# Attention in a fused kernel: 224 instead of 160 columns of one exponential as a polynomial, its value product one pair later

## The chip, the cores and the metric

The kernel runs on one core of a Trainium2 chip. The metric is device time in microseconds (us): the median of three runs before the change is 1327.5 us (1327.15 to 1327.72). A core has TensorE (PE in the profile; PEld is its weight load), VectorE (DVE), ScalarE (ACT), GpSimd (POOL) and SyncE (SP, which here only issues DMAs). SBUF is the working memory, PSUM the memory that matmuls write to.

## The reference, cut to what matters

```python
def reference(A_x, A_wqkv, A_wo, B_x, B_w_gate, B_w1, B_w2, gate_w):
    # a: 16 heads of width 28 over 2048 positions
    scores = jnp.einsum("bhqd,bhkd->bhqk", q, k) * scale
    p = _softmax(scores, axis=-1)
    o = jnp.einsum("bhqk,bhkd->bhqd", p, v)
    a = o.transpose(0, 2, 1, 3).reshape(B, S, D) @ wo
    # b: eight experts, the two best for each position
    b = _B_ref(x, B_w_gate, B_w1, B_w2)
    g = _sigmoid((x * gate_w).sum(-1, keepdims=True))
    return g * a + (1 - g) * b
```

Everything is float32. The change touches only `p` and the product of `p` and `v`.

## The kernel before, in words

The kernel first makes queries, keys and values and routes the positions, then runs the experts (with the row maxima of the scores between), then the attention, then the output projection. The change lies in the attention, which begins at about 829 us of the span and ends at about 1287 us.

**Units and pairs.** Sixteen units `u`, one for each group of four heads and each quarter of 512 queries (`NU = 16`). A unit goes over the 16 tiles of 128 keys in eight pairs `p` (`NPR = 8`). All is numbered by `m = 8u + p`, 0 to 127. The loop (L1377) calls for each `m`: `scores(m + 1)`, `values(m)`, then `beside(m)`, which puts smaller work between: DMAs, splitting the projection's weights (`split_wo_high`, `split_wo_low` in units 5 to 8 at p = 0 to 3), the reciprocals of the row sums, and in the last unit the splitting of the output. A manual schedule holds PE, VectorE, ScalarE and GpSimd to the order in which the code issues; each works through its own queue in that order.

**Scores.** `scores` makes, for both key tiles of a pair and four heads, a 128 x 512 block of scores, in three passes of four matmuls (`score_passes`, L796), the four on different rows of the array. The four blocks of the first tile go to the bank z0 and the three banks s0, those of the second to s1 (three) and z1. PSUM has just these eight banks, and `values` uses z0 and z1 again: its two accumulators are `single(0)` and `single(1)`. So the next scores of the first tile need z0 after the first addition of `values`, and those of the second tile need z1 after the second.

**Exponentials.** Eight blocks of 512 columns for each pair. ScalarE does one from z0 (L1276), three from s0 (L1277) and three from s1 (L1285). The eighth block, z1, is first scaled by VectorE into `X` (L1278); ScalarE then makes the exponential of its first 512 - 160 = 352 columns (L1286), and `power` makes the other 160 as a polynomial: GpSimd forms u, n, g and the exponent bits e (L1292, L1293, L1294, L1297), VectorE y, v, w and the last product (L1301, L1302, L1303, L1305). GpSimd also issues DMAs from the lists `due` and `rows`: of these one comes before e and one behind it.

**Values.** `values(m)` multiplies the eight blocks with the values, first the columns 0 to 287 (`CA = 288`) of all blocks, then 288 to 511, each of the four heads on its own 32 columns of the array: 8 + 8 matmuls (L1319), each of which appears twice in the trace, since float32 takes two instructions. VectorE adds the first part to the unit's sums (`add0` in what follows, L1331, or a copy at p = 0, L1329), then the second (`add1`). Between them stands `piece`: in units 2 to 15 at p = 2 and 3 half of the division of an earlier unit (L1205).

Of the kernel before, what the change touches and what calls it, by code (L numbers as in the profile page):

```python
# [9 lines left out]
F32 = mybir.dt.float32  # L10
# [3 lines left out]
AF = mybir.ActivationFunctionType  # L14
ALU = mybir.AluOpType
# [22 lines left out]
NT = S // 128  # L38
# [12 lines left out]
SCALE = float(DH) ** -0.5  # L51
# [13 lines left out]
def tile_gated_mha_moe(ctx: ExitStack, tc: tile.TileContext, x, xe_, xT, wv, wqk, wo, w1, w2, out):  # L65
    nc = tc.nc
# [31 lines left out]
    DATA = mybir.DependencyInfo(mybir.DependencyClass.Sync, mybir.DependencyReason.DATA)  # L98
# [127 lines left out]
    def whole(n):  # L226
        return -(-n // 32) * 32
# [69 lines left out]
    with ExitStack() as pa:  # L297
        sb = pa.enter_context(tc.tile_pool(name="pa_sb", bufs=1))
# [119 lines left out]
        for t in range(NT):  # L418
# [368 lines left out]
    Ps = {}  # L787
# [13 lines left out]
    with ExitStack() as pb:  # L801
        sb1 = pb.enter_context(tc.tile_pool(name="pb_sb1", bufs=2, reuse_waits="tile"))
        sb = pb.enter_context(tc.tile_pool(name="pb_sb", bufs=2, reuse_waits="tile"))
# [175 lines left out]
        for e in range(E):  # L979
# [11 lines left out]
            for hf in range(2):  # L991
# [3 lines left out]
                for f in range(NH):  # L995
                    ft = hf * NH + f
                    p = e * NP + ft // 2
# [73 lines left out]
                for n_k, k in enumerate((4, 0, 1, 2, 3)):  # L1071
# [7 lines left out]
                    n = min(128, CAPS[e] - k * 128)  # L1079
                    cs = slice(k * 128, k * 128 + n)  # L1080
                    if k < 4:
                        py = accumulator()
                    i = 0
                    for f in range(NH if k < 4 else 0):
                        hh, hl, ht = hs[f]
                        w2h, w2l, w2r = w2t[base + f]
                        for a, b in ((hh, w2h), (hh, w2l), (hl, w2h)):
                            mm = nc.tensor.matmul(py[:n, 0:D], a[:, cs], b, start=i == 0, stop=i == 3 * NH - 1)  # L1088
# [7 lines left out]
                        if hf == 1 and e + 1 < E and (f == 1 or f == 4 and n_k == 1):  # L1096
                            j = n_k if f == 1 and n_k > 1 else f // 4
# [30 lines left out]
    sb = ctx.enter_context(tc.tile_pool(name="pc_sb", bufs=2, reuse_waits="tile"))  # L1128
# [100 lines left out]

    ctx.enter_context(tc.manual_schedule(engines=MANUAL_E))  # L1230
    NPR = NT // 2
    PW = 160
    CA = 288
    ROUND = 1.5 * 2.0 ** 23
    LAM = 0.3125
    EXP2 = (-1.4162444446908184, 1.4393188497873604, 0.43138228078296503, 0.3791024559194178)
    powers = {}
    due, rows = [], []
    NU = 4 * NG
    b1s, halves = {}, {}  # L1240
    accs, rc, rs = {}, {}, {}
    qs = {0: q, 1: load_q(0, 1)}
    held = {0: (kts, v1)}
    Pc = {0: Ps[0] + Ps[1]}

    arrivals = {}
    def behind_values(u, p):
# [4 lines left out]
    def single(i):  # L1252
        return ps.tile([128, 512], F32, name=f"z{i % 2}")
# [9 lines left out]
    def scores(m):  # L1263
        u, p = divmod(m, NPR)
        if p == 0 and u and u + 1 < NU:
            qs[u + 1] = load_q((u + 1) // 4, (u + 1) % 4)
            behind_values(u, 5)
        X = sb.tile([128, 512], F32, name="X")
        P = sb.tile([128, 8, 512], F32, name="P")
        z, t = [None] * 2, [None] * 2  # L1270
        for i in range(2):
            kt = 2 * p + i
            z[i], t[i] = single(i), triple(i)
            three = [t[i][:, j] for j in range(3)]
            score_passes(kt, held[u // 4][0][kt // 8], qs[u], three + [z[i]] if i else [z[i]] + three)
        nc.scalar.activation(P[:, 0], z[0], AF.Exp, scale=SCALE)  # L1276
        nc.scalar.activation(P[:, 1:4], t[0], AF.Exp, scale=SCALE)  # L1277
        nc.vector.tensor_scalar(X, z[1], LAM * SCALE * math.log2(math.e), -126.0 * LAM, op0=ALU.mult, op1=ALU.max)  # L1278
        if m - 1 in powers:
            next(powers.pop(m - 1), None)  # L1280
        w = PW if m + 1 < NU * NPR else 0
        if w:
            powers[m] = power(X[:, 512 - w:], P[:, 7, 512 - w:])
            next(powers[m])
        nc.scalar.activation(P[:, 4:7], t[1], AF.Exp, scale=SCALE)  # L1285
        nc.scalar.activation(P[:, 7, 0:512 - w], X[:, 0:512 - w], AF.Exp, scale=math.log(2.0) / LAM)  # L1286
        Pc[m] = [P[:, i] for i in range(8)]

    def power(x, to):
        u, n, g, y = (sb.tile([128, PW], F32, name=f"p{c}", bufs=1 + (c == "u")) for c in "ungy")  # L1290
        e, v, w = u.bitcast(I32), x, g
        nc.gpsimd.tensor_scalar(u, x, 1.0 / LAM, ROUND, op0=ALU.mult, op1=ALU.add)  # L1292
        nc.gpsimd.tensor_scalar(n, u, -ROUND, LAM, op0=ALU.add, op1=ALU.mult)  # L1293
        nc.gpsimd.tensor_tensor(g, n, x, op=ALU.subtract)  # L1294
        if due:
            due.pop(0)()
        nc.gpsimd.tensor_scalar(e, u, 127.0 - ROUND, 2.0 ** 23, op0=ALU.add, op1=ALU.mult)  # L1297
        if rows:
            rows.pop(0)()
        yield  # L1300
        nc.vector.scalar_tensor_tensor(y, g, EXP2[0], g, op0=ALU.add, op1=ALU.mult)  # L1301
        nc.vector.scalar_tensor_tensor(v, y, EXP2[1], g, op0=ALU.add, op1=ALU.add)  # L1302
        nc.vector.scalar_tensor_tensor(w, y, EXP2[2], v, op0=ALU.add, op1=ALU.mult)  # L1303
        yield
        nc.vector.scalar_tensor_tensor(to, w, EXP2[3], e.bitcast(F32), op0=ALU.add, op1=ALU.mult)  # L1305

    def values(m):
        u, p = divmod(m, NPR)
        P = Pc.pop(m)
        parts = [(single(0), slice(0, CA)), (single(1), slice(CA, 512))]  # L1310
        runs = [(n, i) for n in range(2) for i in range(2)]
        if m + 1 == NU * NPR:
            runs.sort(key=lambda r: r[1])
        for n, i in runs:
            po, cs = parts[n]
            kt = 2 * p + i
            v = held[u // 4][1][kt // 8]
            for j in range(4):
                mm = nc.tensor.matmul(po[32 * j:32 * j + 32, cs], v[:, kt % 8, 32 * j:32 * j + 32],  # L1319
                                      P[4 * i + j][:, cs], start=i == 0, stop=i == 1)  # L1320
                if arrivals.get(m) and (i, j) not in ((0, 0), (1, 3)):
                    tc.add_manual_dep(mm.ins, arrivals[m].pop(0).ins.name, DATA, reason="operands' arrival")
        if p == 0:
            accs[u] = sb.tile([128, 512], F32, name="osb", bufs=4)
        for n, (po, cs) in enumerate(parts):
            if n:
                piece(u, p)
            if p == 0:
                nc.vector.tensor_copy(accs[u][:, cs], po[:, cs])  # L1329
            else:  # L1330
                nc.vector.tensor_tensor(accs[u][:, cs], po[:, cs], accs[u][:, cs], op=ALU.add)  # L1331

    def piece(u, p):
        if u > 1 and p in (2, 3):
            divide_half(u - 2, p - 2)
# [41 lines left out]
    for m in range(NU * NPR):  # L1377
        if m + 1 < NU * NPR:
            scores(m + 1)
        values(m)  # L1380
        u, p = divmod(m, NPR)
        if u + 1 < NU and p in (4, 6):
            rows.append(lambda t=u + 1, c=p // 2 - 2: fetch_routed(t, c))
        if u == 0 and p in (0, 2):
            rows.append(lambda t=u, c=p // 2: fetch_routed(t, c))
        beside(m)
        if m + 1 in powers:
            next(powers[m + 1])
    collect_sums(NU - 1)
    slice_sums(NU - 1)  # L1390
    divide(NU - 2)
# [3 lines left out]
    for t in range(NT):  # L1395
# [67 lines left out]
```

## Time and profile before

| | us |
|---|---|
| median of three runs | 1327.5 |
| lowest, highest | 1327.15, 1327.72 |
| the profiled execution: its own time | 1328.14 |
| its span, first to last instruction | 1326.3 |
| PE, PEld busy | 1321.1, 928.2 |
| VectorE, ScalarE, GpSimd busy | 1068.2, 838.3, 858.1 |

The profiled execution is 0.64 us above the median, and 1.8 us of its time lie outside the span. A row that groups instructions gives the engine, the operation, out<-in by the program's names, the shapes, the count, then the busy time, the mean in ns, and the idle time of the engine just before them with what ended it. A row of the timeline gives the start, the length, the engine, the line, the operation, and in brackets the idle time before it where that is over about 0.2 us. Neighbouring instructions on ScalarE and VectorE overlap by some 0.1 us, so that a wait shorter than that shows as no idle time. The granted clock is 1.0 throughout.

### The profile page before, as it was taken

The page shows a single profiled execution, that of the slowest core. Times are in us where ns is not written, and L with a number is a line of the kernel's source. Part 1 is how long each engine was busy: PE and PEld are TensorE (multiplying, and loading weights), DVE is VectorE, ACT ScalarE, POOL GpSimd, SP SyncE. Part 2 cuts the span into 40 slices and gives each one's busy share as a digit, 9 for nine tenths or more (in the row PEclk, how much of TensorE's full clock was granted, in tenths as well). Part 3 has the DMA queues.
Part 4 walks back from the last instruction along what each step waited for, and adds up shares of the span by engine and source line. Part 5 has one row for each costly group of instructions (what it writes and reads, how often), then busy time and mean ns, then how long its engine had stood idle before and what let it go on. Part 6 is the DMA issues. An engine that isn't in the chain of part 4 may idle for free. (4 is left out here: it accounts for less than half of the span.)

```text
span 1326.3 us, 32115 instructions
## 1 busy us (share of the span) xinstructions
PE 1321.1 (100%) x12210; PEld 928.2 (70%) x12210; DVE 1068.2 (81%) x1686; ACT 838.3 (63%) x1268; POOL 858.1 (65%) x1144
## 2 busy tenths in 40 slices
PE   9999999999999999999999999999999999999999
PEld 8888888788887777777777777555555555555558
DVE  5746898888898888989889886777788887777785
ACT  6316354365354344543444434999999999999981
POOL 2044877777687788786887854666666666666641
PEclk9999999999999999999999999999999999999999
DMA  9888757554553474545745423212422532342214
GB/s 352 291 259 270 212 160 185 154 159 107 169 149 89 148 207 146 165 100 156 187 120 171 106 78 71 56 41 70 115 54 72 118 75 49 75 111 52 51 41 137
DMA packets 138134, 176.65 MB, mean 133 GB/s; under 512 B 24255, under 2 KB 105857, under 8 KB 137465
## 3 DMA queue, kind: packets, MB, share of 16 engines
q1 hardware_dynamic: 119273, 145.58, 36.9%
q0 software_dynamic: 18560, 28.77, 10.5%
q8 instruction: 96, 1.57, 0.5%
q14 instruction: 61, 0.50, 0.1%
q10 hardware_dynamic: 144, 0.23, 0.1%
HBM read 124.51 MB, written 53.18 MB: 134 GB/s over the span
## 5 line engine op out<-in xcount | busy, mean ns | idle before, releaser
L155 DVE TENSOR_REDUCE mp<-pm 128x3 f32<-128x1536 f32 (+1 forms) x300 | 508.3, 1736 | 13.1 <-PE pm L134 12.5
L1319 PE MATMUL z<-P,V 128*32 128x288 f32 x4064 | 246.7, 383 | 0.4 <-ACT P L1276 0.2
L796 PE MATMUL z<-Q,K 29*128 29x512 f32 x762 | 225.7, 424 | 0.0
L796 PE MATMUL s<-Q,K 29*128 29x512 f32 x2286 | 224.9, 424 | 0.0
L1319 PEld LDWEIGHTS z<-P,V 128*32 128x32 f32 x4064 | 107.6, 109 | 132.5 <-ACT P L1276 47.1
L1104 ACT ACTIVATE yo<-acc,cg 128x448 f32<-128x448 f32 x64 | 40.6, 635 | 232.2 <-PE acc L1088 211.1
L867 POOL TENSOR_TENSOR w2l<-w2r,w2h 128x448 fp32r<-128x448 f32 x112 | 130.1, 1162 | 87.6 <-ACT w2h L861 64.7
L1285 ACT ACTIVATE P<-s 128x1536 f32<-128x1536 f32 x127 | 185.6, 1461 | 0.0
L1277 ACT ACTIVATE P<-s 128x1536 f32<-128x1536 f32 x127 | 183.6, 1446 | 0.0
L1088 PE MATMUL acc<-w2h,hh 128*128 128x448 f32 (+2 forms) x448 | 166.9, 373 | 0.3 <-PEq L881 0.3
L1088 PE MATMUL acc<-w2h,hl 128*128 128x448 f32 (+2 forms) x448 | 166.6, 372 | 0.0
L1088 PE MATMUL acc<-w2l,hh 128*128 128x448 f32 (+2 forms) x448 | 165.8, 370 | 0.0
L1035 ACT ACTIVATE hf<-acc 128x512 f32<-128x512 f32 (+8 forms) x154 | 73.7, 478 | 134.7 <-PE acc L1030 125.2
L796 PEld LDWEIGHTS z<-Q,K 29*128 29x128 f32 x762 | 121.7, 184 | 49.7 <-DVE osb L1331 39.4
L148 DVE TENSOR_REDUCE mp<-acc 128x1 f32<-128x512 f32 x131 | 90.2, 689 | 78.4 <-PE pm L134 69.3
L796 PEld LDWEIGHTS s<-Q,K 29*128 29x128 f32 x2286 | 125.6, 184 | 38.7 <-ACT P L1285 32.8
L876 POOL TENSOR_TENSOR hl<-hf,hh 128x512 fp32r<-128x512 f32 (+2 forms) x112 | 144.4, 1289 | 1.1 <-ACT hh L1038 1.1
L1030 PE MATMUL acc<-xeh,w1h 128*128 128x512 f32 (+5 forms) x408 | 136.2, 338 | 0.0
L1030 PE MATMUL acc<-xeh,w1l 128*128 128x512 f32 (+5 forms) x408 | 135.8, 338 | 0.0
L1331 DVE TENSOR_TENSOR osb<-z,osb 128x288 f32<-128x288 f32 x224 | 95.1, 425 | 40.3 <-PE z L1319 30.0
L1278 DVE TENSOR_SCALAR X<-z 128x512 f32<-128x512 f32 x127 | 87.9, 692 | 42.4 <-PE z L796 33.2
L1292 POOL TENSOR_SCALAR pu<-X 128x160 f32<-128x160 f32 x126 | 42.0, 333 | 122.4 <-DVE X L1278 120.9
(239 smaller groups left out, 2824.4 us busy)
## 6 DMA issues: line engine op xcount, KB each, us to landing
w2r<-in_w_dram SPq DMA_DIRECT2D x112, 224.0 KB
w1r<-in_w_dram SPq DMA_DIRECT2D x56, 384.0 KB
x_d<-xf SPq DMA_DIRECT2D x115, 64.0 KB
ys_d<-zero_d SPq DMA_DIRECT2D x32, 224.0 KB
qk_d<-hi SPq DMA_DIRECT2D x28, 256.0 KB
qk_d<-lo SPq DMA_DIRECT2D x28, 256.0 KB
w1r<-in_w_dram SPq DMA_DIRECT2D x112, 64.0 KB
Q<-qk_d SPq DMA_DIRECT2D x64, 112.0 KB
```

The lines of the kernel that those rows point to most:

```text
L148: nc.vector.tensor_reduce(mp[:, o:o + 1], banks[0], axis=AX.X, op=ALU.max)
L155: nc.vector.tensor_reduce(mp[:, (o + lo) % 256:(o + lo) % 256 + hi - lo], pm[h][:, lo - 3 * h:hi - 3 * h], axis=AX.X, op=ALU.max)
L796: nc.tensor.matmul(banks[j], k[rw, kt % 8 // 4, ks], q[rw, c], start=i == 0, stop=i == 2)
L867: nc.gpsimd.tensor_tensor(w2l, w2r, w2h.bitcast(F32), op=ALU.subtract)
L876: nc.gpsimd.tensor_tensor(hl, hf32, hh.bitcast(F32), op=ALU.subtract)
L1030: mm = nc.tensor.matmul(pu[:, 0:HC], a, b[:, cs], start=i == 0, stop=i == len(mms) - 1)
L1088: mm = nc.tensor.matmul(py[:n, 0:D], a[:, cs], b, start=i == 0, stop=i == 3 * NH - 1)
L1277: nc.scalar.activation(P[:, 1:4], t[0], AF.Exp, scale=SCALE)
L1278: nc.vector.tensor_scalar(X, z[1], LAM * SCALE * math.log2(math.e), -126.0 * LAM, op0=ALU.mult, op1=ALU.max)
L1285: nc.scalar.activation(P[:, 4:7], t[1], AF.Exp, scale=SCALE)
L1319: mm = nc.tensor.matmul(po[32 * j:32 * j + 32, cs], v[:, kt % 8, 32 * j:32 * j + 32], P[4 * i + j][:, cs], start=i == 0, stop=i == 1)
L1331: nc.vector.tensor_tensor(accs[u][:, cs], po[:, cs], accs[u][:, cs], op=ALU.add)
```

## The change

The constant `PW` goes from 160 to 224; `CA` stays 288, so that the polynomial columns are now exactly the second part of `values`. They get a tile of their own, `back`. Only the last pair (m = 127) makes them on ScalarE.

- ScalarE's share of the eighth block goes from 352 to 288 columns.
- The four GpSimd and four VectorE operations of `power` are 224 columns wide.
- The value product of `back` of pair m is no longer in `values(m)` but closes the second part of `values(m + 1)`, with the values of the key tile before (`d = -1`). Where `m + 1` begins a unit (p = 0), it goes to free columns of the same bank, and VectorE adds it to the sums of the unit before, on 32 partitions.
- VectorE's steps of the polynomial of pair m, before in `scores` and behind `values` of the pair before, now stand in `values(m)`: y ahead of add0, v between add0 and add1 (behind add1 where `piece` or the addition at p = 0 takes that place), w and the last product behind add1.

```diff
-    PW = 160
-    CA = 288
+    PW = 224
+    CA = 512 - PW
...
-        if m - 1 in powers:
-            next(powers.pop(m - 1), None)
-        w = PW if m + 1 < NU * NPR else 0
-        if w:
-            powers[m] = power(X[:, 512 - w:], P[:, 7, 512 - w:])
+        if m + 1 < NU * NPR:
+            powers[m] = power(X[:, CA:512], back)
             next(powers[m])
-        nc.scalar.activation(P[:, 4:7], t[1], AF.Exp, scale=SCALE)
-        nc.scalar.activation(P[:, 7, 0:512 - w], X[:, 0:512 - w], AF.Exp, scale=math.log(2.0) / LAM)
+        nc.scalar.activation(cells[:, 4:7], t[1], AF.Exp, scale=SCALE)
+        nc.scalar.activation(P[:, 7 * 512:], X[:, 0:CA], AF.Exp, scale=math.log(2.0) / LAM)
+        if m not in powers:
+            nc.scalar.activation(back, X[:, CA:512], AF.Exp, scale=math.log(2.0) / LAM)
...
         nc.vector.scalar_tensor_tensor(y, g, EXP2[0], g, op0=ALU.add, op1=ALU.mult)
+        yield
         nc.vector.scalar_tensor_tensor(v, y, EXP2[1], g, op0=ALU.add, op1=ALU.add)
+        yield
         nc.vector.scalar_tensor_tensor(w, y, EXP2[2], v, op0=ALU.add, op1=ALU.mult)
-        yield
         nc.vector.scalar_tensor_tensor(to, w, EXP2[3], e.bitcast(F32), op0=ALU.add, op1=ALU.mult)
...
+        work = powers.pop(m, None)
+        if work:
+            held_back[m] = P[7][1]
+            next(work)
+        back = held_back.pop(m - 1, None)
...
+            if (n, i) == (1, 0) and back is not None and p == 0:
+                nc.tensor.matmul(po[96:128, 0:PW], held[(u - 1) // 4][1][1][:, NT // 2 - 1, 96:128], back,
+                                 start=True, stop=True)
...
+                terms = [(i, P[4 * i + j][n])]
+                if (n, i, j) == (1, 1, 3):
+                    terms = ([(-1, back)] if back is not None and p else []) + ([] if work else terms)
...
             if n:
-                piece(u, p)
+                if back is not None and p == 0:
+                    whole_ = accs[u - 1][96:128, cs]
+                    nc.vector.tensor_tensor(whole_, po[96:128, 0:PW], whole_, op=ALU.add)
+                elif u > 1 and p in (2, 3):
+                    piece(u, p)
+                elif work:
+                    next(work)
...
+        for _ in work or ():
+            pass
...
         beside(m)
-        if m + 1 in powers:
-            next(powers[m + 1])
```

How this moves VectorE's queue, at the end of unit 0 (a pair like most, then the pair at which unit 1 begins). In the names, `z` is the bank, `osb` the unit's sums, `py` and `pg` are y and g (w lies in g's tile, v in `X`), `pu` holds u and e. Before:

```order
L1278 TENSOR_SCALAR X<-z_10301 128x512
L1305 SCALAR_TENSOR_TENSOR P<-pg,pu 128x160
L1331 TENSOR_TENSOR osb<-z_10330,osb 128x288
L1331 TENSOR_TENSOR osb<-z_10331,osb 128x224
L1301 SCALAR_TENSOR_TENSOR py<-pg 128x160
L1302 SCALAR_TENSOR_TENSOR X<-py,pg 128x160
L1303 SCALAR_TENSOR_TENSOR pg<-py,X 128x160
L1278 TENSOR_SCALAR X<-z_10369 128x512
L1305 SCALAR_TENSOR_TENSOR P<-pg,pu 128x160
L1329 COPY osb<-z_10397 128x288
L1329 COPY osb<-z_10398 128x224
```

The same place in VectorE's queue of the changed kernel, where L1281 is the scaling into `X`, L1303, L1305, L1307 and L1308 are y, v, w and the last product, and L1353, L1351 and L1345 are the additions, the copies and the addition of `back` to the sums of the unit before:

```order
L1281 TENSOR_SCALAR X<-z_10305 128x512
L1303 SCALAR_TENSOR_TENSOR py<-pg 128x224
L1353 TENSOR_TENSOR osb<-z_10334,osb 128x288
L1305 SCALAR_TENSOR_TENSOR X<-py,pg 128x224
L1353 TENSOR_TENSOR osb<-z_10335,osb 128x224
L1307 SCALAR_TENSOR_TENSOR pg<-py,X 128x224
L1308 SCALAR_TENSOR_TENSOR back<-pg,pu 128x224
L1281 TENSOR_SCALAR X<-z_10374 128x512
L1303 SCALAR_TENSOR_TENSOR py<-pg 128x224
L1351 COPY osb<-z_10402 128x288
L1345 TENSOR_TENSOR osb<-z_10403,osb 32x224
L1351 COPY osb<-z_10403 128x224
```

Between X and add0 stands y of the pair before, where the last product of the pair before stood; v has moved between the additions; w and the last product follow add1 and end with the pair.

On PE at the beginning of unit 1, before, with `K` the keys, `V` the values and `Q` the queries:

```order
L796 MATMUL z_10369<-Q,K_7954 128x512
L1319 MATMUL z_10397<-P,V_7963 32x288 x8
L1319 MATMUL z_10398<-P,V_7963 32x224 x8
L796 MATMUL z_10423<-Q,K_7954 128x512
L796 MATMUL s_10424<-Q,K_7954 128x512 x3
```

The same place on PE in the changed kernel:

```order
L796 MATMUL z_10374<-Q,K_7954 128x512
L1335 MATMUL z_10402<-P,V_7963 32x288 x8
L1325 MATMUL z_10403<-back,V_9782 32x224
L1335 MATMUL z_10403<-P,V_7963 32x224 x7
L796 MATMUL z_10430<-Q,K_7954 128x512
```

The second part has seven products of this pair and one of `back`, here at its head; at p over 0 that one stands at its end (`x7`, then one from `back`). The count and the widths of PE's matmuls stay as they were. GpSimd's queue keeps its order.

More of the change, by code (lines that the diff above doesn't have):

```diff
@@ L1243, in tile_gated_mha_moe @@
     held = {0: (kts, v1)}
-    Pc = {0: Ps[0] + Ps[1]}
+    Pc = {0: [(x[:, 0:CA], x[:, CA:512]) for x in Ps[0] + Ps[1]]}
+    held_back = {}
     arrivals = {}
@@ L1268, in scores @@
         X = sb.tile([128, 512], F32, name="X")
-        P = sb.tile([128, 8, 512], F32, name="P")
+        P = sb.tile([128, 7 * 512 + CA], F32, name="P")
+        back = sb.tile([128, PW], F32, name="back", bufs=3)
+        cells = P[:, 0:7 * 512].rearrange("p (c n) -> p c n", n=512)
         z, t = [None] * 2, [None] * 2
@@ L1275, in scores @@
             score_passes(kt, held[u // 4][0][kt // 8], qs[u], three + [z[i]] if i else [z[i]] + three)
-        nc.scalar.activation(P[:, 0], z[0], AF.Exp, scale=SCALE)
-        nc.scalar.activation(P[:, 1:4], t[0], AF.Exp, scale=SCALE)
+        nc.scalar.activation(cells[:, 0], z[0], AF.Exp, scale=SCALE)
+        nc.scalar.activation(cells[:, 1:4], t[0], AF.Exp, scale=SCALE)
         nc.vector.tensor_scalar(X, z[1], LAM * SCALE * math.log2(math.e), -126.0 * LAM, op0=ALU.mult, op1=ALU.max)
-        if m - 1 in powers:
-            next(powers.pop(m - 1), None)
-        w = PW if m + 1 < NU * NPR else 0
-        if w:
-            powers[m] = power(X[:, 512 - w:], P[:, 7, 512 - w:])
-            next(powers[m])
-        nc.scalar.activation(P[:, 4:7], t[1], AF.Exp, scale=SCALE)
-        nc.scalar.activation(P[:, 7, 0:512 - w], X[:, 0:512 - w], AF.Exp, scale=math.log(2.0) / LAM)
-        Pc[m] = [P[:, i] for i in range(8)]
+        if m + 1 < NU * NPR:
+            powers[m] = power(X[:, CA:512], back)
+            next(powers[m])
+        nc.scalar.activation(cells[:, 4:7], t[1], AF.Exp, scale=SCALE)
+        nc.scalar.activation(P[:, 7 * 512:], X[:, 0:CA], AF.Exp, scale=math.log(2.0) / LAM)
+        if m not in powers:
+            nc.scalar.activation(back, X[:, CA:512], AF.Exp, scale=math.log(2.0) / LAM)
+        Pc[m] = [(c[:, 0:CA], c[:, CA:512]) for c in (cells[:, i] for i in range(7))] + [(P[:, 7 * 512:], back)]
     def power(x, to):
-        u, n, g, y = (sb.tile([128, PW], F32, name=f"p{c}", bufs=1 + (c == "u")) for c in "ungy")
+        u, n, g, y = (sb.tile([128, PW], F32, name=f"p{c}", bufs=1 + (c in "ug")) for c in "ungy")
         e, v, w = u.bitcast(I32), x, g
@@ L1315, in values @@
             po, cs = parts[n]
-            kt = 2 * p + i
-            v = held[u // 4][1][kt // 8]
+            if (n, i) == (1, 0) and back is not None and p == 0:
+                nc.tensor.matmul(po[96:128, 0:PW], held[(u - 1) // 4][1][1][:, NT // 2 - 1, 96:128], back,
+                                 start=True, stop=True)
             for j in range(4):
[L1319 to L1322, printed above, removed]
+                terms = [(i, P[4 * i + j][n])]
+                if (n, i, j) == (1, 1, 3):
+                    terms = ([(-1, back)] if back is not None and p else []) + ([] if work else terms)
+                last = i == 1 or (n, j) == (1, 3) and work and not (back is not None and p)
+                for k, (d, x) in enumerate(terms):
+                    kt = 2 * p + d
+                    v = held[u // 4][1][kt // 8]
+                    mm = nc.tensor.matmul(po[32 * j:32 * j + 32, cs], v[:, kt % 8, 32 * j:32 * j + 32], x,
+                                          start=i == 0, stop=bool(last) and k + 1 == len(terms))
+                    if arrivals.get(m) and (i, j) not in ((0, 0), (1, 3)):
+                        tc.add_manual_dep(mm.ins, arrivals[m].pop(0).ins.name, DATA, reason="operands' arrival")
         if p == 0:
```

## The prediction

> **What bounds the kernel now.** I read the busy time of the engines over the attention first: from pair 3 to pair 121, one window (us, then busy PE, PEld, VectorE, ScalarE, GpSimd, clock, DMA share, GB/s).
>
> ```profile
> 836.61:1259.87 423.26, 422.89 (x6612) 217.98 (x6612) 334.89 (x883) 422.79 (x474) 269.92 (x558) 1.00 0.31 72
> ```
>
> These are 118 pairs, 3.587 us each. PE and ScalarE are both full, so busy time doesn't tell which of them sets the pace. The chain of waits, in order of time, from 900 to 960 us, gives PE 94%:
>
> ```profile
> by line: PE z L1319 48.7%; PE s L796 26.1%; PE z L796 19.3%; DVE X L1278 1.2%; issue 1.1%; POOL pg L1294 0.9%; DVE osb L1329 0.8%; DVE py L1301 0.6%; DVE X L1302 0.6%; POOL pn L1293 0.6%; DVE pg L1303 0.5%; POOLq L1294 0.0%
> ```
>
> That chain prefers an engine that never shows a gap, so I tested it where ScalarE would show the opposite, in two neighbouring pairs of the timeline. First PE's own rows: the third score pass into z0, after which z0 is complete.
>
> ```profile
> 929.31 0.38 PE L796 MATMUL z<-Q,K 28*128 28x512 f32 x1
> ...
> 932.91 0.38 PE L796 MATMUL z<-Q,K 28*128 28x512 f32 x1
> ```
>
> Then ScalarE's: its last exponential of a pair (L1286, the one that the change shortens) and its first of the next (L1276, which reads z0).
>
> ```profile
> 929.39 0.51 ACT L1286 ACTIVATE P<-X 128x352 f32<-128x352 f32 x1
> 929.78 0.60 ACT L1276 ACTIVATE P<-z 128x512 f32<-128x512 f32 x1
> ...
> 932.93 0.51 ACT L1286 ACTIVATE P<-X 128x352 f32<-128x352 f32 x1
> 933.38 0.60 ACT L1276 ACTIVATE P<-z 128x512 f32<-128x512 f32 x1
> ```
>
> L1276 starts 0.39 us after L1286 in the first pair and 0.45 in the second, but 0.47 after PE's third pass in both. A ScalarE that ran at its own limit would keep its own spacing; it keeps PE's. So the exponential of z0 waits for PE, by less than the 0.1 us that neighbouring ScalarE instructions overlap (929.39 + 0.51 reaches beyond 929.78), and therefore without a visible gap.
>
> One whole pair, p = 2 of unit 5, the fullest kind. PE, from the values of one pair to those of the next:
>
> ```profile
> 980.97 1.94 PE L1319 MATMUL z<-P,V 128*32 128x288 f32 x32
> 982.84 0.50 PE L796 MATMUL z<-Q,K 29*128 29x512 f32 x1
> ...
> 983.41 0.39 PE L796 MATMUL z<-Q,K 28*128 28x512 f32 x1
> ...
> 983.66 0.49 PE L796 MATMUL z<-Q,K 29*128 29x512 f32 x1
> ...
> 984.22 0.38 PE L796 MATMUL z<-Q,K 28*128 28x512 f32 x1
> ...
> 984.55 0.45 PE L1319 MATMUL z<-P,V 128*32 128x288 f32 x4
> ```
>
> PE's steps: both value parts 1.87 (980.97 to 982.84), the first tile's passes up to its third 0.57, to the second tile 0.25, to its third pass 0.56, to the next values 0.33: 3.58 us, the whole pair. A second loop of nearly the same length runs through ScalarE, which frees the second tile's banks with L1285:
>
> ```profile
> 982.13 1.46 ACT L1285 ACTIVATE P<-s 128x1536 f32<-128x1536 f32 x1
> ```
>
> It ends at 983.59, and the second tile's scores start 0.07 later. In this loop are L1276, L1277 and L1285; L1286 is in neither.
>
> VectorE in the same pair, with a division half in the slot between the additions (L1205) and a split of the projection's weights behind them (L1145):
>
> ```profile
> 981.19 0.69 DVE L1278 TENSOR_SCALAR X<-z 128x512 f32<-128x512 f32 x1 [0.25 <-PE z L796]
> 981.80 0.32 DVE L1305 SCALAR_TENSOR_TENSOR P<-pg,pu 128x160 f32<-128x160 f32 x1
> 982.21 0.46 DVE L1331 TENSOR_TENSOR osb<-z,osb 128x288 f32<-128x288 f32 x1
> 982.59 0.42 DVE L1205 TENSOR_TENSOR osb<-osb,rs 128x256 f32<-128x256 f32 x1
> 983.00 0.39 DVE L1331 TENSOR_TENSOR osb<-z,osb 128x224 f32<-128x224 f32 x1
> 983.31 0.38 DVE L1145 TENSOR_TENSOR wo_l<-wo_r,wo_h 128x224 fp32r<-128x224 f32 x1
> 983.61 0.43 DVE L1301 SCALAR_TENSOR_TENSOR py<-pg 128x160 f32<-128x160 f32 x1
> 984.08 0.33 DVE L1302 SCALAR_TENSOR_TENSOR X<-py,pg 128x160 f32<-128x160 f32 x1
> 984.44 0.33 DVE L1303 SCALAR_TENSOR_TENSOR pg<-py,X 128x160 f32<-128x160 f32 x1
> ```
>
> **The change part by part.** The durations, from the groups of the same window, shapes apart:
>
> ```profile
> L1277 ACT ACTIVATE P<-s 128x1536 f32<-128x1536 f32 x118 | 170.6, 1446 | 0.0
> ...
> L1276 ACT ACTIVATE P<-z 128x512 f32<-128x512 f32 x119 | 71.2, 598 | 0.5 <-ACT P L1286 0.5
> L1294 POOL TENSOR_TENSOR pg<-pn,X 128x160 f32<-128x160 f32 x118 | 64.5, 547 | 9.9
> L1286 ACT ACTIVATE P<-X 128x352 f32<-128x352 f32 x119 | 60.5, 508 | 0.0
> L1297 POOL TENSOR_SCALAR pu<-pu 128x160 int32<-128x160 f32 x118 | 49.7, 421 | 9.6
> L1331 DVE TENSOR_TENSOR osb<-z,osb 128x288 f32<-128x288 f32 x104 | 47.6, 458 | 11.0 <-PE z L1319 1.0
> ...
> L1331 DVE TENSOR_TENSOR osb<-z,osb 128x224 f32<-128x224 f32 x104 | 40.8, 392 | 25.7 <-PE z L1319 25.7
> ...
> L1292 POOL TENSOR_SCALAR pu<-X 128x160 f32<-128x160 f32 x118 | 39.2, 332 | 114.2 <-DVE X L1278 112.9
> L1302 DVE SCALAR_TENSOR_TENSOR X<-py,pg 128x160 f32<-128x160 f32 x119 | 38.7, 325 | 4.1
> L1293 POOL TENSOR_SCALAR pn<-pu 128x160 f32<-128x160 f32 x118 | 38.2, 324 | 9.7
> ...
> L1142 DVE CAST wo_h<-wo_r 128x224 fp32r<-128x224 f32 x8 | 3.4, 420 | 0.0
> ```
>
> *ScalarE, 64 columns less.* From 512 to 1536 columns a column costs (1446 - 598) / 1024 = 0.83 ns, so L1286 loses 53 ns, in 126 pairs 6.7 us of ScalarE's time. On the path that is nothing: the next instruction waits for z0. What it buys is slack of 0.05 a pair.
>
> *PE.* The same matmuls, and those of `back` stand beside those of the other heads as before: nothing. Its operand is a pair old when it is read. At p = 0 the product of `back` stands at the head of the second part; were it to run alone, its two instructions would cost as much as two of the 32 in 1.87 us, 0.12 in each of 15 pairs, 1.8 us. I take nothing, as the count on each of the four column groups stays.
>
> *GpSimd, four wider operations.* At most in proportion, 0.4 x (547 + 421 + 332 + 324) = 0.65 us a pair. Its busy time is 269.92 / 118 = 2.29 a pair with all its DMAs; 2.94 is still under 3.58. y now stands ahead of add0, so that a late g would hold add0, and behind it PE's scores into z0. But y is wanted a pair later than g is made: g ended here at 983.39, and y would stand 0.61 behind the next X, at 985.38, with 2.0 us of room for the 0.65. What that removes is bounded by VectorE's waits for g, in the same window:
>
> ```profile
> DVE py L1301 <- POOL pg L1294: 4.1, 11, 0.4
> ```
>
> That is 4.1 us in 11 pairs, nearly all in front of an X that waited for PE anyway (0.25 idle before X in the quoted pair). I take 0.2 us of 0 to 0.9; 0.9 is all that 126 pairs have above 3.58.
>
> *VectorE.* A column costs (458 - 392) / 64 = 1.03 ns, so each of the four operations grows by 66 ns, 0.26 a pair. What matters is where. From X (0 at 981.19): add0 stands at 1.02, held by PE's first value part. y in the place of the last product begins at 0.61 and takes 0.39: it ends at 1.00, add0 stays; if y were longer, PE would feel it only beyond the 0.17 between add0's end (982.67) and PE's scores into z0 (982.84). In the slot v begins like the division half, at 1.40, and ends at 1.79; add1 stands at 1.81, and PE wants z1 0.27 after add1's end (983.39 to 983.66). Behind add1 the next operation starts at 2.12. At p = 2 and 3 (28 pairs), and at p = 0 (15), where the addition on 32 partitions has the slot and costs about add1's 0.39, v, w and the last product follow there. Dependent ones are 0.36 apart at 160 columns (984.08 to 984.44), so 0.42 at 224: at 2.12, 2.54 and 2.96, and 0.30 later, at 3.26, the queue is free for the next X, due at 3.58. The cover is 0.32 there and 0.74 in all other pairs. In eight pairs L1145 comes behind, 0.30: 3.56, just covered. In four it is L1142, 420 ns: 3.60. Twelve pairs may thus be late by 0 to 0.03: I take 0.2 us in all.
>
> GpSimd works beside these operations now, as it did beside L1205 and L1301 of the quoted pair:
>
> ```profile
> 982.79 0.60 POOL L1294 TENSOR_TENSOR pg<-pn,X 128x160 f32<-128x160 f32 x1
> 983.48 0.39 POOL L1297 TENSOR_SCALAR pu<-pu 128x160 int32<-128x160 f32 x1
> ```
>
> Bound below: L1205 beside L1294 took its 0.42, so nothing. Bound above: the quoted L1301 beside L1297 took 0.43, where such an operation has 0.32: 0.11 each. I take the lower end, since the division half with its two SBUF inputs is nearest to v and w in kind; both ends go to the range.
>
> *The ends.* The last pair has its eighth block in two ScalarE instructions, 0.1 us more at most, partly given back as the first part starts earlier. I take nothing.
>
> *The sum.* -0.2 + 0.2 = 0. The profiled execution took 1328.14, of which 1326.3 is span; the sum of nothing holds for it as for the median, 0.64 lower. **Forecast: 1327.5 us.** A measurement of this kernel can tell about 0.2%, 2.7 us, from no change.
>
> **The rivals.**
>
> *ScalarE sets the pace.* Then 126 x 53 ns go: 1320.8. For it speaks ScalarE's 422.79 of 423.26 us; against it that L1276 follows PE and not L1286 in time. The Trainium skill, Perfetto Trace Analysis, Identifying the Most-Contended Engine, holds matmul busy time to be no measure, names weight-load busy time for TensorE (here 217.98 of 423.26) and occupancy for ScalarE, and calls the fullest engine the one to improve: by that rule the time would be this rival's 1320.8; the spacing of 0.47 in both pairs doesn't agree with it. Chance 0.07.
>
> *ScalarE sets it in the fast pairs only.* Where L1276 stood 0.39 behind L1286, both may have released it. If every second pair falls by up to 0.05 and its neighbour doesn't give it back: 63 x 0.05 = 3.2, 1324.3. Against it: the short spacing is followed by a long one, so that the pairs' sum is set elsewhere. Chance 0.07.
>
> *VectorE runs over its pair,* the one on the other side. Its queue is free for X at 3.26, and the slower engine would be VectorE where v, w and the last product take 0.11 more each, as L1301 did beside GpSimd: 3.59 in 31 pairs and up to 3.89 in twelve, 31 x 0.01 + 12 x 0.31 = 4.0 us: 1331.5. It decides from 0.11 on without a split behind, at once with one; X is then late, and behind it the second value part. For it: the profile shows no pair with these operations over GpSimd's n and g. Against it: L1205's 0.42. Chance 0.09.
>
> *The two engines shut each other out.* The same place, but whole waits: v for n, w for g, the last product for e, at 1.4 times their durations at most 0.45 + 0.77 + 0.59 = 1.8 us, of which I take half, 0.9. The queue would be free 0.58 late in 43 pairs and 0.16 late in the other 83: 38 us, 1366. The Trainium skill, SBUF — State Buffer, Who interferes with whom, says this of a VectorE instruction with two SBUF inputs beside a GpSimd one that reads SBUF. By that rule the time would be that 1366; the trace doesn't agree: L1205 ran on beside L1294, which took 0.60 for its mean 0.547. Chance 0.03.
>
> **How the numbers follow.** Forecast 0.74, its own range 1326.6 (0.9 gained) to 1328.5 (twelve pairs late by 0.08). The range reaches down to the fast pairs' 1324.3 and up to the overrun's 1331.5, and leaves out the first and the last rival, 0.10, and strays beyond these ends. Faster by over 0.2%: 0.07 + 0.07 = 0.14. Slower: 0.09 + 0.03 = 0.12. Within: 0.74.
>
> **What would show it.** In the changed profile L1286's 288 columns take about 455 ns, but the exponential of z0 still starts 0.39 to 0.45 behind it and 0.47 behind PE's third pass, so that ScalarE's busy time falls by up to 6 us while PE stays full; the pair stays at 3.58 to 3.59. VectorE's three-input operations take about 0.39, and X follows PE. Wrong it would be if that distance shrank to 0.34 and the pair fell to 3.53, or if X in the pairs with p = 0, 2 and 3 waited for VectorE itself.

## The result, and the profile after

| | before | after |
|---|---|---|
| median, us | 1327.61 | 1344.36 |
| lowest, highest | 1327.15, 1328.2 | 1343.85, 1344.85 |
| span of the profiled execution | 1326.3 | 1342.3 |
| PE, PEld busy | 1321.1, 928.2 | 1330.5, 935.0 |
| VectorE, ScalarE, GpSimd busy | 1068.2, 838.3, 858.1 | 1124.1, 839.3, 897.1 |

The ratio is 1.0123 (95% interval 1.0108 to 1.0138): the change makes the kernel slower, by 16.8 us. The forecast was no change. The granted clock stays 1.0. All line numbers below are those of the changed kernel, where nothing else is said.

The attention in one window (us, then busy PE, PEld, VectorE, ScalarE, GpSimd, clock, DMA share, GB/s):

```profile
836.61:1270.00 433.39, 427.39 (x6560) 222.42 (x6560) 384.21 (x889) 420.31 (x469) 303.37 (x554) 1.00 0.30 71
```

ScalarE had 0.5 us free in its window before and now has 13; PE had 0.4 and now has 6.0. VectorE went from 79% to 89%, and as will be seen a part of that is waiting that its records count as work. I measured the pairs themselves as the distance from one exponential of z0 to the next, 126 of them in each trace: their mean went from 3.589 to 3.712 us, 15.5 us in all, of the 16.0 us by which the spans differ. The median pair only went from 3.581 to 3.597. So a few pairs lose nearly all of it (a pair's delay shows in the stretch behind it):

| stretches, from z0's exponential to the next | count | more than before, us | mean now, us |
|---|---|---|---|
| right behind the values of p = 0 | 16 | +8.74 | 4.15 |
| right behind the values of p = 2 and 3 in units 5 to 8 | 8 | +4.52 | 4.14 |
| the rest of the last unit | 5 | +0.91 | 3.78 |
| all others | 97 | +1.32 | 3.60 |

Of the first sixteen, the one in unit 0, which has no addition of `back`, loses nothing.

First the undisturbed pairs. ScalarE's last exponential of a pair (L1286) and the first of the next (L1279), in two neighbouring pairs:

```profile
905.30 0.46 ACT L1286 ACTIVATE P<-X 128x288 f32<-128x288 f32 x1
906.06 0.60 ACT L1279 ACTIVATE P<-z 128x512 f32<-128x512 f32 x1 [0.30 <-PE s L796]
...
909.21 0.46 ACT L1286 ACTIVATE P<-X 128x288 f32<-128x288 f32 x1
909.62 0.60 ACT L1279 ACTIVATE P<-z 128x512 f32<-128x512 f32 x1
```

PE's third score pass into z0, of the same pairs:

```profile
905.58 0.39 PE L796 MATMUL z<-Q,K 28*128 28x512 f32 x1
...
909.14 0.38 PE L796 MATMUL z<-Q,K 28*128 28x512 f32 x1
```

L1279 starts 0.48 behind PE's pass in both, although it stands 0.76 behind L1286 in the first and 0.41 in the second: it follows PE, as before.

Now the durations, from the groups of instructions between 840 and 1270 us, shapes apart (count | busy us, mean ns of one | idle just before, and what ended it):

```profile
L1296 POOL TENSOR_TENSOR pg<-pn,X 128x224 f32<-128x224 f32 x117 | 80.4, 687 | 9.7
...
L1307 DVE SCALAR_TENSOR_TENSOR pg<-py,X 128x224 f32<-128x224 f32 x117 | 63.2, 540 | 1.4
L1305 DVE SCALAR_TENSOR_TENSOR X<-py,pg 128x224 f32<-128x224 f32 x116 | 60.2, 519 | 0.4
L1286 ACT ACTIVATE P<-X 128x288 f32<-128x288 f32 x117 | 53.2, 455 | 0.0
L1308 DVE SCALAR_TENSOR_TENSOR back<-pg,pu 128x224 f32<-128x224 f32 x116 | 48.0, 414 | 12.5 <-POOL pu L1299 0.5
...
L1303 DVE SCALAR_TENSOR_TENSOR py<-pg 128x224 f32<-128x224 f32 x116 | 44.2, 381 | 0.0
L1345 DVE TENSOR_TENSOR osb<-z,osb 32x224 f32<-32x224 f32 x14 | 5.6, 397 | 4.5 <-PE z L1335 4.5
```

y (L1303) takes 381 ns and the last product (L1308) 414, near the 0.39 that was forecast. But v (L1305) takes 519 and w (L1307) 540 for the same number of columns, with next to no idle time in front of them. One pair shows why: p = 2 of unit 5, the pair that the prediction used. VectorE, from the division half to the next X:

```profile
989.66 0.41 DVE L1205 TENSOR_TENSOR osb<-osb,rs 128x256 f32<-128x256 f32 x1
990.16 0.39 DVE L1353 TENSOR_TENSOR osb<-z,osb 128x224 f32<-128x224 f32 x1
990.47 0.84 DVE L1305 SCALAR_TENSOR_TENSOR X<-py,pg 128x224 f32<-128x224 f32 x1
991.35 0.39 DVE L1307 SCALAR_TENSOR_TENSOR pg<-py,X 128x224 f32<-128x224 f32 x1
991.84 0.47 DVE L1308 SCALAR_TENSOR_TENSOR back<-pg,pu 128x224 f32<-128x224 f32 x1
992.24 0.38 DVE L1145 TENSOR_TENSOR wo_l<-wo_r,wo_h 128x224 fp32r<-128x224 f32 x1
992.54 0.68 DVE L1281 TENSOR_SCALAR X<-z 128x512 f32<-128x512 f32 x1
```

and GpSimd beside it:

```profile
989.70 0.62 POOL L1295 TENSOR_SCALAR pn<-pu 128x224 f32<-128x224 f32 x1
990.39 0.67 POOL L1296 TENSOR_TENSOR pg<-pn,X 128x224 f32<-128x224 f32 x1
```

v is on record from 990.47, while GpSimd's g runs from 990.39 to 991.06. v ends at 991.31, 0.25 behind g, and 224 columns at the prediction's 1.03 ns are 0.23: v did its work after g and stood still before. w, the last product and the split of weights follow, and X starts with no idle time in front of it: it waits for VectorE.

Over the attention the same holds case by case. Of the 126 v, 58 began while n was in flight and 43 while g was; those that were lengthened ended 234 to 239 ns after n or 244 to 253 after g, however long they had waited, and the longest took 886. Another 23 v began about 0.03 us ahead of n, and there it was n that was lengthened. Of the 126 w, 80 began beside g; their median is 556 ns and they end 244 to 254 after g. The 30 w that began beside nothing of GpSimd's take 380 to 394.

The second kind of late pair, p = 0 of unit 4. VectorE:

```profile
946.87 0.69 DVE L1281 TENSOR_SCALAR X<-z 128x512 f32<-128x512 f32 x1 [0.44 <-PE z L796]
947.48 0.38 DVE L1303 SCALAR_TENSOR_TENSOR py<-pg 128x224 f32<-128x224 f32 x1
947.90 0.46 DVE L1351 COPY osb<-z 128x288 f32<-128x288 f32 x1
948.68 0.40 DVE L1345 TENSOR_TENSOR osb<-z,osb 32x224 f32<-32x224 f32 x1 [0.32 <-PE z L1335]
949.09 0.39 DVE L1351 COPY osb<-z 128x224 f32<-128x224 f32 x1
949.51 0.49 DVE L1305 SCALAR_TENSOR_TENSOR X<-py,pg 128x224 f32<-128x224 f32 x1
...
950.53 0.61 DVE L1308 SCALAR_TENSOR_TENSOR back<-pg,pu 128x224 f32<-128x224 f32 x1
951.07 0.68 DVE L1281 TENSOR_SCALAR X<-z 128x512 f32<-128x512 f32 x1
```

and PE's scores of the second tile, first those into s1, in a row that groups them with the last into s0, then the first into z1:

```profile
949.10 0.73 PE L796 MATMUL s<-Q,K 28*128 28x512 f32 x5
949.63 0.46 PE L796 MATMUL z<-Q,K 29*128 29x512 f32 x1
```

The addition on 32 partitions (L1345) does not start in the slot 1.40 behind X. It waits, in the bracket, for PE's values, and starts 1.81 behind X, where the copy of the second part would have started. The copy comes 0.41 later, and it is the copy that gives z1 back to PE, whose scores into z1 start at 949.63, right behind the copy's end at 949.48. Those into s1 start at 949.34, 0.29 ahead; the distance is 0.29 to 0.30 at all fifteen p = 0 from unit 1 on. In the kernel before, the two start together, within 0.02 us at the same fifteen places; at p = 0 of unit 4:

```profile
947.50 0.50 PE L796 MATMUL s<-Q,K 29*128 29x512 f32 x3
947.51 0.49 PE L796 MATMUL z<-Q,K 29*128 29x512 f32 x1
```

In the changed kernel v, w and the last product come later too, and the next X stands 4.20 behind the last.

### The profile page after: what moved, and what is told of

Read it like the earlier page. It is cut to its first block, busy times and chain, and to the rows that moved or that the text cites. A ratio compares the mean times of both kernels' runs of the same rounds, so it can differ in the third digit from the quotient of the medians.

```text
span 1342.3 us, 32016 instructions
## 1 busy us (share of the span) xinstructions
PE 1330.5 (99%) x12210; PEld 935.0 (70%) x12210; DVE 1124.1 (84%) x1701; ACT 839.3 (63%) x1269; POOL 897.1 (67%) x1144
## 5 line engine op out<-in xcount | busy, mean ns | idle before, releaser
L1335 PE MATMUL z<-P,V 128*32 128x288 f32 x3810 | 251.5, 385 | 7.2 <-DVE X L1281 5.5
L1294 POOL TENSOR_SCALAR pu<-X 128x224 f32<-128x224 f32 x126 | 55.7, 442 | 99.9 <-DVE X L1281 97.9
L835 POOL TENSOR_TENSOR w1l<-w1r,w1h 128x1024 fp32r<-128x1024 f32 (+1 forms) x49 | 91.0, 1857 | 41.1 <-issue 18.8
L1281 DVE TENSOR_SCALAR X<-z 128x512 f32<-128x512 f32 x127 | 87.3, 687 | 32.8 <-PE z L796 25.2
```

What stands on the lines that cost most here:

```text
L835: nc.gpsimd.tensor_tensor(l[:, :, half], r[:, :, half], h[:, :, half].bitcast(F32), op=ALU.subtract)
```

## The experiments

Each was compared with runs of the kernel before made beside it (1327.34 to 1327.62). Two theories stood against each other at first: that v and w, beside GpSimd's n, g and e, make VectorE late; and that the width, or the cut of ScalarE, or the addition at p = 0 is the cause.

**a_wide**: only the width, in the kernel before.

```diff
-    PW = 160
+    PW = 224
```

> The kernel before with 224 polynomial columns and nothing else: the old order, the product in its own pair. Theory (the cost is where the wider polynomial now stands: its VectorE steps lie beside GpSimd's steps of the next pair, and each waits for the GpSimd operation in flight to end): in the old order y, v and w follow the pair's own g, so no such waits, but g comes about 0.35 us later and the three steps take 0.42 each, so that VectorE's queue is free for X only 0.07 late (more if y meets e): 126 x 0.07 = 9 us, about 1336, up to 1380 where y always waits for e. Rival (the 224 columns alone make the 17 us, the order adds nothing): 1344. Rival (the width is harmless, the new order alone costs): 1327.5.

Measured: 1358.95 us, ratio 1.024 (1.0223 to 1.0257), 23 above the 1336 of the expectation, whose bound of 1380 was for a wait of y for e. Here nearly all pairs are longer, 3.83 us in the mean, and the wait that ends last is another. VectorE's wait of y (here L1301) for g (L1294), between 840 and 1270 us (us in total, times, longest):

```profile
DVE py L1301 <- POOL pg L1294: 36.2, 88, 0.8
```

In the old order y is wanted right after g, and GpSimd's three wider steps are too long for that. The relaxed order does remove this wait: the changed kernel, with the same width, is 14.6 us faster than this one. In the kernel before that wait came to 4.1 us in 11 pairs, so that there was little for the new order to win against 160 columns.

**b_narrow**: the changed kernel's order at 160 columns.

```diff
+    PC = 160
...
-            powers[m] = power(X[:, CA:512], back)
+            powers[m] = power(X[:, 512 - PC:], eighth[:, 512 - PC:])
...
-        nc.scalar.activation(P[:, 7 * 512:], X[:, 0:CA], ...
+        nc.scalar.activation(eighth[:, 0:512 - w], X[:, 0:512 - w], ...
```

> The changed kernel with the new order and the product a pair later, but 160 polynomial columns (ScalarE again makes 352): Theory: the steps stay beside GpSimd's, but the waits are shorter (n 0.32, g 0.55) and v, w and the last product 0.07 each; at p = 0 the queue is free at about 4.3 after the pair's L1279 where 4.46 is due, so only units 5 to 8 and 15 stay late: 1328 to 1331. Rival (the order alone costs, whatever the width): 1344. Rival (the addition at p = 0 alone, with its wait for the second part): the 8.7 us of the pairs after p = 0 stay, 1336.

Measured: 1333.5, ratio 1.0048 (1.0031 to 1.0065), 2.5 above the expectation. The splits' pairs are back at +0.30 us, but those behind p = 0 still lose 3.85. So with 160 columns the first kind of late pair is gone and the second is not, and my theory of p = 0 lacked something.

**c_behind**: the addition at p = 0 behind the copy, v in the slot.

```diff
-                if back is not None and p == 0:
-                    whole_ = accs[u - 1][96:128, cs]
-                    nc.vector.tensor_tensor(whole_, po[96:128, 0:PW], whole_, op=ALU.add)
-                elif u > 1 and p in (2, 3):
+                if u > 1 and p in (2, 3):
...
+        if back is not None and p == 0:
+            whole_ = accs[u - 1][96:128, CA:512]
+            nc.vector.tensor_tensor(whole_, parts[1][0][96:128, 0:PW], whole_, op=ALU.add)
```

> The changed kernel with the addition of the earlier unit's back product moved behind add1, so that v stands in the slot at p = 0 too. Theory (that addition waits for the whole second value part, since both lie in one bank, and everything behind it starts 0.4 late): the 8.7 us of the pairs after p = 0 fall to 1 or 2, 1336 to 1338. Rival (only the waits for GpSimd count): under 2 us gained, 1342 to 1344.

Measured: 1338.51, ratio 1.0084 (1.0067 to 1.0101), just above the expected band. Behind p = 0 the loss falls from 8.74 to 4.73 us: the place of the addition matters. Not its place alone: z1's scores still start 0.29 to 0.41 behind s1's at all fifteen p = 0.

**d_nogp**: without GpSimd's four operations; VectorE's four keep their widths and read X and y in the place of g and e.

```diff
-        e, v, w = u.bitcast(I32), x, g
-        nc.gpsimd.tensor_scalar(u, x, ...
-        nc.gpsimd.tensor_scalar(n, u, ...
-        nc.gpsimd.tensor_tensor(g, n, x, op=ALU.subtract)
-        nc.gpsimd.tensor_scalar(e, u, ...
+        e, v, w, g = y, x, g, x
...
```

> The changed kernel without GpSimd's four polynomial operations (VectorE's four keep their widths and their two operands in SBUF, and read X and y in the place of g and e; the polynomial's value is therefore another). Theory (waits for GpSimd's operations make the cost): VectorE's steps all take 0.39, the eight pairs with a split of the projection's weights fit again, the pairs after p = 0 are late by about 0.1: 1328 to 1331. Rival (the addition at p = 0 makes most of it): the 8.7 us stay, 1336. Rival (VectorE's own width): 1344.

Measured: 1333.7, ratio 1.005 (1.0033 to 1.0066). VectorE's three steps, v, w and the last product, in its groups:

```profile
L1304 DVE SCALAR_TENSOR_TENSOR back<-pg,py 128x224 f32<-128x224 f32 x119 | 46.7, 392 | 4.1
L1303 DVE SCALAR_TENSOR_TENSOR pg<-py,X 128x224 f32<-128x224 f32 x119 | 45.8, 385 | 1.4
...
L1301 DVE SCALAR_TENSOR_TENSOR X<-py,X 128x224 f32<-128x224 f32 x118 | 45.2, 383 | 0.5
```

All 126 v now take 379 to 394 ns, and the splits' pairs lose 0.05 us instead of 4.52 and the rest of the last unit nothing instead of 0.91. The time missed the expectation by nearly 3 us. It lies behind p = 0, where 4.53 remain, 0.30 at each of fifteen, for the 0.1 expected.

**e_cut**: the kernel before with 288 columns on ScalarE; columns 288 to 351 of the eighth block are left out and hold a constant, written beforehand into two fixed tiles (`Pk`).

```diff
...
-        P = sb.tile([128, 8, 512], F32, name="P")
+        P = Pk[m % 2]
...
-        nc.scalar.activation(P[:, 7, 0:512 - w], X[:, 0:512 - w], ...
+        nc.scalar.activation(P[:, 7, 0:CA if w else 512], X[:, 0:CA if w else 512], ...
```

> The kernel before, in its own order and with 160 polynomial columns, but ScalarE makes 288 columns of the eighth block, not 352; the 64 columns between are left out (a constant stands there). Theory (ScalarE's last exponential lies on no path, the exponential of z0 waits for PE): 1327.5, at most 0.9 less. Rival (ScalarE sets the pace): 1320.8. Rival (in the fast pairs only): 1324.3.

Measured: 1328.49, ratio 1.0009 (1.0 to 1.0018). The prediction's window:

```profile
836.61:1259.87 423.26, 422.63 (x6600) 217.45 (x6596) 334.00 (x880) 422.16 (x471) 269.43 (x557) 1.00 0.31 72
```

ScalarE still looks full, although 53 ns of its work are gone from each pair: its rows overlap, and waits under 0.1 us hide there. Both rivals that wanted a gain, 1320.8 and 1324.3, fall. The Trainium skill, Perfetto Trace Analysis, Identifying the Most-Contended Engine, would take this row as a sign that ScalarE is the engine to improve; the run doesn't agree, with 1328.49 for 1327.62.

**f_bank**: the product of `back` at p = 0 in z0's bank, from which VectorE can take it earlier.

```diff
-            if (n, i) == (1, 0) and back is not None and p == 0:
-                nc.tensor.matmul(po[96:128, 0:PW], ...
+            if (n, i) == (0, 0) and back is not None and p == 0:
+                nc.tensor.matmul(po[96:128, CA:512], ...
...
-                    nc.vector.tensor_tensor(whole_, po[96:128, 0:PW], whole_, op=ALU.add)
+                    nc.vector.tensor_tensor(whole_, parts[0][0][96:128, CA:512], whole_, op=ALU.add)
```

> The changed kernel, but at p = 0 the back product goes to free columns of the first part's bank and is the first product of that part, and its addition stays in the slot between the additions. Theory (the addition waited for the whole second part because it read that part's bank): it now starts right behind the first addition, at about 2.28 instead of 2.68 after L1279, the pairs after p = 0 lose most of their 8.7 us and keep about 2 (the waits for GpSimd and the four pairs with a split): 1337 to 1340. Rival (it is the extra instruction, not its wait): 1343 to 1344.

Measured: 1345.9, ratio 1.0137 (1.0122 to 1.0153): nothing gained. The stretches behind p = 0 fell to +0.26 us in all, but the ones just before them rose to 4.28 us each. VectorE, p = 0 of unit 2:

```profile
890.68 0.46 DVE L1351 COPY osb<-z 128x288 f32<-128x288 f32 x1 [0.37 <-PE z L1335]
891.15 0.40 DVE L1345 TENSOR_TENSOR osb<-z,osb 32x224 f32<-32x224 f32 x1
```

and PE's next scores into z0:

```profile
891.69 0.47 PE L796 MATMUL z<-Q,K 29*128 29x512 f32 x1 [0.65 <-DVE osb L1345]
```

PE waits 0.65 us for the addition by name. What the addition does is now plain: it holds a bank that PE wants next, whichever of the two it reads.

**h_both**: d_nogp and c_behind together.

> The changed kernel without GpSimd's four polynomial operations (as in the run that left them out, the polynomial's value is another) and with the addition of back behind add1. Theory (the waits for GpSimd and the wait for the bank are all of it, the widths cost nothing by themselves): 1328 to 1330. Rival (a third cost): stays at 1331 or above.

Measured: 1332.57, ratio 1.0038 (1.0025 to 1.0051), again above. Behind p = 0 there remain 3.43 us. VectorE's copy of the second part and the addition behind it, p = 0 of unit 2:

```profile
889.63 0.39 DVE L1344 COPY osb<-z 128x224 f32<-128x224 f32 x1
890.03 0.40 DVE L1349 TENSOR_TENSOR osb<-z,osb 32x224 f32<-32x224 f32 x1
```

and PE's first score into z1:

```profile
890.58 0.46 PE L796 MATMUL z<-Q,K 29*128 29x512 f32 x1
```

Ahead of the copy or behind it, z1 is free only after both, at 890.43, and PE's score starts 0.15 later, again 0.28 to 0.30 behind s1's in all fifteen. Whether anything else is left in this pair without GpSimd, m_nogp_noadd shows below.

**i_narrow_bank**: b_narrow with f_bank's edit.

> 160 polynomial columns in the new order, the product a pair later, and the back product at p = 0 in the first part's bank. Theory: both costs are gone or covered: 1327.5 to 1329.5, and no faster than before, since PE's own steps fill the pair. Rival (without the stalls, the relaxed order shows a gain): 1325 or below.

Measured: 1339.03, ratio 1.0086 (1.0073 to 1.01). Missed for f_bank's reason: z0 is held, the pairs with p = 0 take 4.27 us.

**m_nogp_noadd**: d_nogp without the addition at p = 0.

```diff
-                    nc.vector.tensor_tensor(whole_, po[96:128, 0:PW], whole_, op=ALU.add)
+                    pass
```

> The changed kernel without GpSimd's four polynomial operations, and with the addition of back at p = 0 left out as well (its product is still made, nobody adds it). Theory (two costs: waits for GpSimd, and an extra addition that holds z1 about 0.29 longer, so that the second tile's scores into z1 start late): nothing of both is left, 1328 to 1330. Rival (a third cost in the pairs after p = 0, such as VectorE's widths): stays at 1332 or above.

Measured: 1328.62, ratio 1.0012 (1.0003 to 1.0022). Behind p = 0 nothing is lost (-0.27 us), nor behind the splits (0.09), and z1's scores again start within 0.02 us of s1's. The product of `back` is still made at p = 0, so that it costs nothing.

**n_noadd**: the changed kernel without that addition, GpSimd working.

> The changed kernel with the addition of back at p = 0 left out (the product is made, nobody adds it); GpSimd's operations as they are. Theory: the pairs after p = 0 lose most of their 8.7 us, the pairs with a split of the projection's weights keep theirs (4.5 us, and four more of that kind at p = 0): 1335 to 1338. Rival (the addition counts only where nothing else is late): above 1340.

Measured: 1337.54, ratio 1.0077 (1.0062 to 1.0093): the splits' pairs keep their loss (4.9 us), those behind p = 0 keep 2.09.

**o_narrow_noadd**: b_narrow without that addition.

> 160 columns in the new order, the product a pair later, the addition at p = 0 left out. Theory: 3.9 us of the 5.9 that this width still cost were the addition's hold on z1, so 1329 to 1330, and no faster than the kernel before, since PE's own steps fill the pair. Rival (free of stalls, the relaxed order gains): 1325 or below.

Measured: 1329.95, ratio 1.0024 (1.0015 to 1.0033). At 160 columns the later product and the relaxed order, without their addition, gain nothing over the kernel before; they are about 2.6 us slower, and the cause of that was not sought.

**k_write**: GpSimd keeps its place in the pair, but after one operation on eight columns, which waits for X, it only writes: five memsets of the same tiles.

```diff
-        nc.gpsimd.tensor_scalar(u, x, 1.0 / LAM, ROUND, op0=ALU.mult, op1=ALU.add)
-        nc.gpsimd.tensor_scalar(n, u, ...
-        nc.gpsimd.tensor_tensor(g, n, x, op=ALU.subtract)
+        nc.gpsimd.tensor_scalar(u[:, 0:8], x[:, 0:8], 1.0 / LAM, ROUND, op0=ALU.mult, op1=ALU.add)
+        nc.gpsimd.memset(u[:, 8:], 1.0)
+        nc.gpsimd.memset(n, 1.0)
+        nc.gpsimd.memset(g, 0.5)
+        nc.gpsimd.memset(n, 1.0)
...
-        nc.gpsimd.tensor_scalar(e, u, ...
+        nc.gpsimd.memset(u, 1.0)
```

> The changed kernel with GpSimd's four operations replaced by one of 8 columns that reads X, and five memsets of the same tiles, which read nothing (values are constants; VectorE's operations are unchanged and read the same tiles). Theory (VectorE with two operands in SBUF is kept out only by a GpSimd operation that reads SBUF): VectorE's steps take 0.39 throughout, as in the run without GpSimd's operations: 1332 to 1335. Rival (any GpSimd operation keeps it out): steps of 0.5 and longer where a memset is in flight, 1338 or above.

Measured: 1334.24, ratio 1.0054 (1.0038 to 1.0069), d_nogp's time. In its timeline GpSimd writes, and v (here L1307) begins beside it:

```profile
962.06 0.28 POOL L1297 MEMSET pg<- 128x224 f32 x1
962.14 0.38 DVE L1307 SCALAR_TENSOR_TENSOR X<-py,pg 128x224 f32<-128x224 f32 x1
962.28 0.27 POOL L1298 MEMSET pn<- 128x224 f32 x1
```

v takes its 0.38 and ends at 962.52, between the ends of the two writes. In all, 89 v began beside one of the memsets and take 380 to 393 ns. The memsets are short, 0.28 us, but 17 of the 89 had 0.19 us or more of one left: ending 0.24 behind it, as they do behind n, they would have taken 0.43 or longer. The tiles that VectorE reads and writes are those of the changed kernel, so that a wait for other data does not explain the difference. So it is not GpSimd's being busy that holds VectorE, but its operations that read SBUF. The Trainium skill, SBUF — State Buffer, Who interferes with whom, says that a VectorE operation with two SBUF inputs and a GpSimd one that reads SBUF block each other, that a pure write does not, and that whoever issues first holds the other. The runs agree in all three: w ends 244 to 254 ns after g, v runs its 383 beside memsets, and before the change g was the one that waited beside L1205.

**The sum.** The two causes, taken out one after the other:

| kernel | us | step |
|---|---|---|
| changed | 1344.36 | |
| GpSimd's reads out (d_nogp) | 1333.7 | -10.7 |
| addition out too (m_nogp_noadd) | 1328.62 | -5.1 |
| before, run beside it | 1327.34 | -1.3 |

In the other order the addition gives 6.8 (n_noadd) and GpSimd 8.9: some 1.7 us belong to both at once, since they meet behind p = 0. About 1.3 us is not assigned. No version here is faster than the kernel before.

## Why the prediction was wrong, point by point

The sum had 0.2 us for VectorE and nothing for what its operations and their reads hold up. Two of its steps failed, worth 8.9 to 10.7 and 5.1 to 6.8 us by the runs, by the order in which they are taken out.

**PE sets the pace and ScalarE's cut is worth nothing: right.** e_cut shows it alone, 1.0009, and after the change L1279 still stands 0.48 behind PE's third pass.

**GpSimd's width and the 2.0 us of room for y: right.** y takes 381 ns and no longer shows a wait for g, where a_wide's y waits for g 36.2 us in all.

**VectorE's widths: right where it is undisturbed,** 381 to 392 ns beside the 0.39 forecast.

**The step that failed first: the bound for v, w and the last product beside GpSimd.** The prediction said "L1301 beside L1297 took 0.43, where such an operation has 0.32: 0.11 each. I take the lower end", so nothing. Read again, the quoted rows say more. L1297 ran from 983.48 to 983.87, L1301 from 983.61 to 984.04. It ended 0.17 behind L1297, and 160 columns at 1.03 ns are 0.165: it had stood still until L1297 ended, and did all its work after it. The trace before has 39 such cases of y, v and w, lengthened to between 0.34 and 0.44, and every one ends 0.17 to 0.18 behind L1297. The 0.11 was not a price of working side by side but what happened to be left of a wait. The lower end was mis-read too: L1205 began at 982.59, L1294 at 982.79, and the one that began later paid. All 28 g of that trace that began beside a division half end 0.38 to 0.39 behind it and take 574 to 700 ns, where the 98 others take 523 to 537; the mean of 547 had mixed the two. So "the trace doesn't agree", which the prediction held against the rival of the two engines, was wrong: its own rows agreed. They show one rule, that the later starter waits, and I took it for two prices of one effect. In the new order v and w start while n and g are in flight in most pairs, and are mostly the later ones. Their means are 137 and 155 ns over the 0.38, the largest single delay about 0.5.

**The rivals.** "The two engines shut each other out" had the mechanism, and "VectorE runs over its pair" the place; they had 0.12 between them. The first was over-priced at 1366: it charged each pair 0.9, and its 83 pairs without extra work lose next to nothing (97 stretches, 1.32 us), since the means are only 0.3 over in all and the cover of 0.74 holds. In eight pairs with a split, where the cover was forecast as nearly nothing, it costs 4.52 / 8 = 0.57 each.

**The step that failed second: the addition at p = 0.** The prediction gave it the slot, from 1.40 behind X, at 0.39. It reads z1's bank, and starts only when the second part is complete, 1.81 behind X; and as a second reader of that bank it gives the bank back about 0.4 us later, of which 0.29 reaches PE. Fifteen times 0.29 are 4.4 of the 5.1 us that went with the addition in m_nogp_noadd. That PE's own work at p = 0 costs nothing was right; but I had costed the addition on VectorE only, without asking who waits for what it reads. b_narrow, d_nogp, f_bank, h_both and i_narrow_bank all came out above their bands, by 2.5 to 9.5 us, because my theory still lacked the hold on the bank.

**The sign named as "wrong if" is the one that came,** but not in all the pairs named: X waits for VectorE itself at the fifteen p = 0 and at the eight p = 2 and 3 with a split, where it stands 0.68 to 1.28 and 1.18 to 1.24 us behind PE's last score pass into z1, for about 0.54 elsewhere. At most of the other p = 2 and 3 it is late by 0.1 or not at all.

## What to carry to other kernels

When a neighbouring engine's row is a little longer than its mean, put the ends side by side before you call it a price: an operation that ends just the time of its own columns after another's end has waited for it, and the next time the wait can be nearly as long as the other operation is. Before moving a VectorE operation with two SBUF inputs, ask which GpSimd operations that read SBUF will be in flight when it starts; and for each new reader of an accumulator's bank, ask when that bank is complete and who wants it next.

## What the runs showed of the hardware that I had not expected

- A VectorE operation that is held by GpSimd is on record from before its wait: the wait is in its duration (0.84 us for 0.38) and nearly none in its idle time (0.4 us before 116 v together). The groups show it as a slow instruction.
- The hold is exact: the lengthened operations of 224 columns end 234 to 254 ns after the GpSimd operation's end, whatever they waited. So an operation that starts with less than some 0.14 us of the other left shows nothing: 48 last products began beside e with 0.14 us or less of it left and took 391 to 395 ns.
- GpSimd is held in the same way: in the 23 cases where v began about 0.03 us before n, n took 582 to 586 ns instead of 377.
- A memset of the same size on GpSimd holds nothing: the median of 89 v is 381 ns, against 516 beside n and 555 beside g, which read SBUF.
